# Two-phase MLPs after an attention: token and weight pieces queued half a step apart, some made a phase earlier

## The chip, the cores and the metric

The kernel runs on one core of one Trainium2 chip. The metric is the device time of one execution in microseconds (us). A core has the engines TensorE (PE, whose weight loads are listed as PEld), VectorE (DVE), ScalarE (ACT), GpSimd (POOL) and SyncE (SP). Each engine takes its own instructions in the order in which the program emits them, and here every DMA is issued by SP.

## The reference

Three stages follow each other. First comes an attention over 4 batches, 8 heads, 576 positions and 64 columns a head, with a bias that a small MLP makes from relative positions. Then two MLPs of 2304 tokens, 512 model columns and 2048 hidden columns, without residuals, all in float32:

```python
def _moe_ref(x, w_in, w_out):                 # layer 0
    h = x @ w_in
    g = h - np.tanh(h)
    return (g @ w_out).astype(np.float32)

def _moe2_ref(x, w_in, w_out, s, b):          # layer 1
    h = x @ w_in
    r = np.maximum(h, 0.0)
    g = s * (r * r) + b
    return (g @ w_out).astype(np.float32)
```

## The kernel before

Every instruction order is written out by hand: what is emitted first on an engine runs first there. A tile taken from a pool waits, in its first instruction, until the slot's last user is done.

**Attention** runs in 80 periods (`periods`, `NK`), one for a pair of heads, a batch and a block of 128 rows. In a period's end stand extra pieces from the table `work`: the weight steps of layer 0 for blocks u = 0 and 1 (`WK`, `WP`) and the tokens of batch 0 (`XK`, `XP`).

**First products.** Hidden columns are cut into 8 blocks (u) of 256, tokens into 4 batches (b) of 576. One pair (u, b) is an item. An item multiplies 2x2 blocks by Strassen's scheme with seven products P1 to P7 of 288 columns. Each product adds six matmuls: two halves j of the contraction, and three combinations of a high and a low part (a float32 is split into a rounded high part and the rest, hence "hi" and "lo", the second made by a subtraction). `first` gives two functions: `part0` emits P1, P6, P7 and the copy of P1 on ACT (L338) and two sums on DVE (L340, L342); `part1` emits P5, P2, P4, P3, the sums c22, c21 and c12 on DVE, the gates (`gate`, `gate2`) and two stores of g to DRAM (L362) on SP. Sums and gates live in the tile `ring`, a pool of 11 slots of 576 columns; products take turns in eight PSUM banks.

**Weights.** `step(layer, m, i)` makes one weight piece in five functions: `fetch` (SP loads 512 KB into the tile `stg`, three slots), `a` (ACT scales the high words, L108; DVE masks the sign, L109, into `wsg`), `b` (two DVE merges, L115 and L117, the last reader of `stg`), `c` (four DVE subtractions of 128 columns in the tile `wx`, for first weights only) and `d` (ACT writes the high part, POOL the low part; tiles `w` for first weights, `v` for second weights).

**Tokens.** `tokens(layer, b, j, e0, e1)` loads half j of a batch (L282), makes three more planes by subtraction (`s1`, `s2`, into the one slot of `xs`) and splits seven planes into high and low parts (tile `x`).

**Second products.** g is read back in 5 chunks of tokens (four of 512, one of 256); for each of 16 slices f, `load_g` (L594) loads 256 KB into a ring tile four steps ahead, `split_g` makes high (ACT, L600) and low parts two steps ahead into the pool `gp` of 14 slots, and `second` emits 12 matmuls (L620). In chunk 0 the low parts are POOL's, in the others DVE's. Second weights are made in the same steps, a slice each. After a chunk four banks are copied into ring tiles and stored (L624, L626).

The list `items` has, for each layer, 32 items and then 80 steps of second products; `pre[n]` lists the pieces emitted ahead of entry n. For a first-product entry, the first half of that list is emitted before `part0` and the second half between `part0` and `part1`. All pieces of a token half stand in one entry, those of batch b in entries 2b-2 and 2b-1 of the layer.

Of the kernel before, what the change touches and what calls it, by code (L numbers as in the profile page):

```python
# [10 lines left out]
F32 = mybir.dt.float32  # L11
# [17 lines left out]
NU = 8  # L29
# [21 lines left out]
XP = [("load", 0), ("s1", 2), ("h0", 3), ("h1", 4), ("l0", 4), ("l1", 5), ("l2", 6), ("s2", 7), ("h2", 7), ("l3", 8)]  # L51

GL, GS = 4, 2

@with_exitstack
def tile_kernel(ctx, tc, qk, vd, wcat, wts, sb, ltab, psib, ipsi8, out):
# [6 lines left out]
    wsg = ctx.enter_context(tc.tile_pool(name="wsg", bufs=1))  # L63
# [27 lines left out]
    raw_w, w1_t, w2_t, w2pool = {}, {}, {}, []  # L91

    def step(layer, m, i):
# [8 lines left out]
        def a():  # L102

            x = wst.tile([128, 8, 128], F32, tag="wx", name="wx")
            sg = wsg.tile([128, 512], I32, tag="wsg", name="wsg")
            hw = raw_w[key][:, 1]
            y = x[:, 0:4].rearrange("p n c -> p (n c)")
            nc.scalar.activation(out=y, in_=hw.bitcast(F32), func=AF.Copy, scale=2.0 ** -112)  # L108
            nc.vector.tensor_scalar(out=sg, in0=hw, scalar1=-2 ** 31, scalar2=1, op0=ALU.bitwise_and, op1=ALU.bitwise_or)  # L109
            raw_w[key] = (raw_w[key], x, y.bitcast(I32), sg)  # L110
# [9 lines left out]
        def c():  # L120
            x = raw_w[key][1]
            if m == 0:
                for o, y, z, op in ((4, 0, 3, ALU.add), (6, 1, 0, ALU.subtract), (5, 4, 1, ALU.subtract), (7, 2, 5, ALU.subtract)):
                    tt(nc.vector, x[:, o], x[:, y], x[:, z], op)

        def d():
# [5 lines left out]
            else:  # L132
                w = w2pool[i == NF - 1].tile([128, 2, 4, 128], F32R, tag=f"v{i}", name=f"v{i}")
# [134 lines left out]
    x_t, xpool, banks = {}, [xb0, None, None, None], []  # L268
# [4 lines left out]
    def tokens(layer, b, j, e0, e1):  # L273
# [3 lines left out]
        def load():  # L277
            r.append(xst.tile([128, 5, HT], F32, tag="xs", name="xs"))
            r.append(xpool[b].tile([128, 2, 7, HT], F32R, tag=f"x{b}{j}", name=f"x{b}{j}"))
            x_t[layer, b, j] = r[1]  # L280
# [15 lines left out]

        def lo(a, c, o, eng):
# [454 lines left out]
```

## Time and profile before

| | us |
|---|---|
| median of 2 runs (1314.87 to 1316.55) | 1315.71 |
| the profiled execution | 1315.19 |
| its span, first to last instruction | 1313.4 |
| PE busy | 1135.5 (86%) |
| DVE busy | 767.0 (58%) |
| ACT busy | 584.9 (45%) |
| POOL busy | 450.7 (34%) |

The stages of the span: bias table to 48 us, attention to 315.6, layer 0's items 1 to 31 to 587.4 (item 0 runs inside the end of attention), layer 0's second products to 811.3, layer 1's items to 1086.6 and its second products to 1309.8. A row of the timeline gives start, duration, engine, line, operation, the written tile, the read tiles, the shape and the count of instructions merged into it; in brackets stands the idle time before it and what ended it. `L85` is a helper that records all two-input operations, so these are told apart by tile. `PEclk` is the clock that TensorE was granted, as a share of the higher of its two levels.

### The profile page before, as it was taken

Reading aid. Unit: us, or ns where it says so; the run is one execution under the profiler, and the core shown is the slowest. Engines: PE = TensorE matmul, PEld = TensorE weight load, DVE = VectorE, ACT = ScalarE, POOL = GpSimd, SP = SyncE. Lnnn points to the kernel's source line nnn. Section 1 sums busy time; section 2 is a strip of 40 time slices with the busy share of each in tenths; the row PEclk is TensorE's granted clock in tenths of the full one; section 3 lists DMA queues with packets and bytes.
Section 4 is the critical chain, followed back from the end, with each engine's and each line's share of the span. In section 5 each row is a group of like instructions: output and inputs, shape, how many; then the busy total and the mean of one; then the engine's idle time right before and its main releaser. Section 6 shows DMA issues by size and latency. Waiting matters only on the chain. (4 is left out here: it accounts for less than half of the span.)

```text
span 1313.4 us, 21145 instructions
## 1 busy us (share of the span) xinstructions
PE 1135.5 (86%) x7624; PEld 901.3 (69%) x7624; DVE 767.0 (58%) x1598; ACT 584.9 (45%) x1178; POOL 450.7 (34%) x526
## 2 busy tenths in 40 slices
PE   9999999997546888888899998555888897799998
PEld 6455555555446888876588888445888796578887
DVE  8777777664235767787754322335778787832222
ACT  8877777773223333333433222222555464432122
POOL 0366566562335444557611110222211116700000
PEclk9999999999667999998999999776999998999999
DMA  8745353421213333465454313321333355444122
GB/s 285 246 128 206 111 189 106 147 84 59 101 56 102 124 122 105 139 202 186 154 192 178 130 35 114 104 72 59 116 139 123 123 195 193 156 161 160 60 85 96
DMA packets 81384, 175.36 MB, mean 134 GB/s; under 512 B 9472, under 2 KB 18560, under 8 KB 81280
## 3 DMA queue, kind: packets, MB, share of 16 engines
q1 hardware_dynamic: 81280, 174.01, 38.8%
q8 instruction: 60, 0.98, 0.3%
q14 instruction: 44, 0.36, 0.1%
HBM read 111.16 MB, written 62.82 MB: 132 GB/s over the span
## 5 line engine op out<-in xcount | busy, mean ns | idle before, releaser
L313 PE MATMUL h<-x,w 128*128 128x288 f32 x1356 | 226.2, 319 | 71.9 <-ACT ring L338 39.1
L313 PE MATMUL a<-x,w 128*128 128x288 f32 x1332 | 217.5, 315 | 67.9 <-ACT ring L338 39.0
L313 PEld LDWEIGHTS h<-x,w 128*128 128x128 f32 x1356 | 207.4, 209 | 81.1 <-ACT ring L338 42.0
L313 PEld LDWEIGHTS a<-x,w 128*128 128x128 f32 x1332 | 199.9, 205 | 75.9 <-ACT ring L338 41.8
L85 DVE TENSOR_TENSOR g<-ring,g 128x512 fp32r<-128x512 f32 (+1 forms) x128 | 87.0, 693 | 122.9 <-ACT g L600 122.5
L600 ACT CAST g<-ring 128x512 fp32r<-128x512 f32 (+1 forms) x160 | 90.0, 575 | 133.3 <-PE h L620 51.5
L452 POOL TENSOR_SCALAR pn<-p,sm 128x576 f32<-128x576 f32 (+2 forms) x208 | 125.2, 618 | 61.8 <-DVE sm L443 41.3
L85 POOL TENSOR_TENSOR w<-wx,w 128x896 fp32r<-128x896 f32 x32 | 67.8, 2122 | 191.6 <-ACT w L136 111.7
L620 PE MATMUL h<-v,g 128*128 128x512 f32 x432 | 118.3, 403 | 13.6 <-ACT g L600 7.9
L421 DVE CUSTOM_DVE_ANT_0 raw<-s,bias 128x576 f32<-128x576 f32 x144 | 103.9, 753 | 44.0 <-PE s L413 38.2
L620 PE MATMUL a<-g,v 128*128 128x512 f32 (+1 forms) x432 | 112.5, 389 | 14.5 <-POOL g L85 7.6
L85 DVE TENSOR_TENSOR ring<-h,ring 128x288 f32<-128x288 f32 x161 | 72.7, 455 | 84.4 <-ACT ring L338 45.4
L620 PE MATMUL h<-g,v 128*128 128x512 f32 (+1 forms) x528 | 121.2, 368 | 0.0
L85 DVE TENSOR_TENSOR ring<-a,ring 128x288 f32<-128x288 f32 x159 | 71.9, 455 | 78.7 <-ACT ring L338 37.4
L620 PE MATMUL a<-v,g 128*128 128x512 f32 x432 | 115.4, 401 | 0.0
L85 POOL TENSOR_TENSOR ring<-ring 128x576 f32<-128x576 f32 x64 | 74.5, 1184 | 116.2 <-ACT ring L318 54.7
L435 ACT ACTIVATE p<-raw,mn 128x576 f32<-128x576 f32 x144 | 110.6, 771 | 4.8 <-POOL pn L452 2.3
L620 PEld LDWEIGHTS h<-v,g 128*128 128x128 f32 x432 | 81.3, 190 | 40.4 <-ACT g L600 11.2
L620 PEld LDWEIGHTS a<-g,v 128*128 128x128 f32 x432 | 78.7, 189 | 38.0 <-POOL g L85 11.5
L620 PEld LDWEIGHTS h<-g,v 128*128 128x128 f32 x528 | 91.7, 190 | 17.9
L620 PEld LDWEIGHTS a<-v,g 128*128 128x128 f32 x432 | 82.6, 191 | 19.6
L462 PEld LDWEIGHTS t<-ident,pn 128*128 128x128 f32 (+1 forms) x656 | 69.7, 140 | 38.3 <-issue 20.6
(66 smaller groups left out, 1535.7 us busy)
## 6 DMA issues: line engine op xcount, KB each, us to landing
g_d<-ring SPq DMA_DIRECT2D x128, 288.0 KB, 2.5
stg<-in_wts SPq DMA_DIRECT2D x64, 512.0 KB, 4.0
ring<-g_d SPq DMA_DIRECT2D x128, 256.0 KB, 5.3
qk<-in_qk SPq DMA_DIRECT2D x16, 864.0 KB, 5.6
bias_d<-m SPq DMA_DIRECT2D x36, 296.0 KB, 4.5
bias<-bias_d SPq DMA_DIRECT2D x32, 288.0 KB, 4.7
xs<-x_d SPq DMA_DIRECT2D x32, 288.0 KB, 3.5
vv<-in_vd SPq DMA_DIRECT2D x16, 320.0 KB, 3.3
```

The source lines that it names most:

```text
L85: eng.tensor_tensor(out=out, in0=a, in1=b, op=op)
L313: nc.tensor.matmul(o, w[:, l, a], x[:, k, c], start=not add and j == 0 and m == 0, stop=j == 1 and m == 2, skip_group_check=add)
L421: nc.vector.tensor_tensor_reduce(out=raw.rearrange("p (c j) -> p c j", c=2), in0=s_t.pop((x, j))[:, :, 0:288], in1=bias_t[pairs[i][0], k]. ...
L435: nc.scalar.activation(out=p, in_=raw, func=AF.Exp, scale=-1.0, bias=mn, accum_out=sm[:, j:j + 1])
L452: nc.gpsimd.tensor_scalar(out=pn[:, c:c + b - a], in0=p[:, a:b], scalar1=sm[:, j:j + 1], scalar2=0.0, op0=ALU.mult, op1=ALU.add)
L462: nc.tensor.transpose(pm[0:c, j - g], pn[:, j * 128:j * 128 + c], ident)
L600: nc.scalar.copy(gh, g)
L620: nc.tensor.matmul(o, x, y, start=f == 0 and j == 0, stop=f == NF - 1 and j == 2)
```

## The change

Pieces are emitted at half steps: `pre[2n]` ahead of entry n, `pre[2n+1]` between `part0` and `part1`. Token pieces are fewer and larger (one `s`, two high parts, two low parts), one half step apart; the two subtracted planes that need extra room are put into a ring tile; `xs` has two slots. Half j = 0 of a batch is DVE's, j = 1 POOL's. Batch 1 of layer 0 is loaded and subtracted in attention's last periods, batches 0 and 1 of layer 1 are made whole, and batch 2 loaded and subtracted, in layer 0's second products. First weights for u = 2 are made up to `c` ahead of their layer, with `d` at half step 14 of it.

In a weight step the sign mask is written in place (it now follows ACT's reading of the same words), `wsg` is gone, the four subtractions of `c` are POOL's, two second-weight pieces share one `wx` tile, and `stg` has two slots; the last second-weight tile stands in a slot of `stg`.

Layer 1's gates are all a Relu on ACT, a square (DVE for "a", POOL for "b" and "c") and a scaling on POOL. High and low parts of g take ring tiles in place of the pool `gp`; loads of g go three steps ahead; in chunk 0 the low parts of odd f are DVE's.

```diff
-WK = [(0, 8), (1, 17), (2, 26), (3, 35)]
+WK = [(0, 8), (1, 17), (2, 26), (3, 35), (4, 52), (5, 60)]
-XK = [(0, 44), (1, 70)]
+XK = [(0, 63), (1, 71)]
+XP = {"load": 0, "s": 2, "h0": 3, "l0": 4, "h1": 5, "l1": 6}
-GL, GS = 4, 2
+GL, GS = 3, 2
...
-    stg = ctx.enter_context(tc.tile_pool(name="stg", bufs=3))
+    stg = ctx.enter_context(tc.tile_pool(name="stg", bufs=2))
-    xst = ctx.enter_context(tc.tile_pool(name="xst", bufs=1))
+    xst = ctx.enter_context(tc.tile_pool(name="xst", bufs=2))
...
-            x = wst.tile([128, 8, 128], F32, tag="wx", name="wx")
-            sg = wsg.tile([128, 512], I32, tag="wsg", name="wsg")
+            if m == 0 or i % 2 == 0:
+                x = w2x[0] = wst.tile([128, 8, 128], F32, tag="wx", name="wx")
+            else:
+                x = w2x[0][:, 4:8]
...
-            nc.vector.tensor_scalar(out=sg, in0=hw, scalar1=-2 ** 31, scalar2=1, op0=ALU.bitwise_and, op1=ALU.bitwise_or)
+            nc.vector.tensor_scalar(out=hw, in0=hw, scalar1=-2 ** 31, scalar2=1, op0=ALU.bitwise_and, op1=ALU.bitwise_or)
...
-                    tt(nc.vector, x[:, o], x[:, y], x[:, z], op)
+                    tt(nc.gpsimd, x[:, o], x[:, y], x[:, z], op)
...
+        def s():
+            x = r[0]
+            r.append(ring().rearrange("p (n c) -> p n c", n=2))
+            tt(eng, x[:, 4], x[:, 1], x[:, 0], ALU.subtract)
+            tt(eng, x[:, 1], x[:, 3], x[:, 1], ALU.subtract)
+            tt(eng, r[1][:, 1], x[:, 3], x[:, 4], ALU.subtract)
+            tt(eng, r[1][:, 0], r[1][:, 1], x[:, 2], ALU.subtract)
...
-                if name == "a":
-                    tt(nc.vector, g, h, g, ALU.mult)
-                nc.scalar.activation(out=g, in_=g, func=AF.Identity, scale=sb_t[:, 0:1], bias=sb_t[:, 1:2])
+                tt(nc.vector if name == "a" else nc.gpsimd, g, g, g, ALU.mult)
+                nc.gpsimd.tensor_scalar(out=g, in0=g, scalar1=sb_t[:, 0:1], scalar2=sb_t[:, 1:2], op0=ALU.mult, op1=ALU.add)
...
-            gh, gl = (gpool[0].tile([128, 512], F32R, tag="g", name="g")[:, 0:cn] for _ in range(2))
+            gh, gl = (ring(F32R)[:, 0:cn] for _ in range(2))
-            tt(nc.vector if c else nc.gpsimd, gl, g, gh.bitcast(F32), ALU.subtract)
+            tt(nc.vector if c or f % 2 else nc.gpsimd, gl, g, gh.bitcast(F32), ALU.subtract)
...
+            for q, (b, j) in enumerate((b, j) for b in range(2 + layer, B) for j in range(2)):
+                t = tokens(layer, b, j, (nc.vector, nc.gpsimd)[j])
+                for f, k in (("load", 0), ("s", 1), ("h0", 2), ("l0", 3), ("h1", 2), ("l1", 3)):
+                    add(2 * a0 + 2 + q // 2 * 4 + j + k, t[f])
...
+            for u in range(3, NU):
+                k = 2 * a0 + 8 * (u - 1)
+                for j, at in enumerate(((-6, -2, 0, 1, 3), (-3, 1, 3, 4, 6))):
+                    t = step(layer, 0, 2 * u + j)
+                    for f, n in zip(("fetch", "a", "b", "c", "d"), at):
+                        add(max(k + n, 2 * a0 + 14) if u == 3 and f == "a" else k + n, t[f])
...
+                    at = [2 * (f - n) for n in (5, 3, 2, 1)]
+                for p, n in zip(("fetch", "a", "b", "d"), at):
+                    order.append((k + n, "dba fetch".index(p), t[p]))
...
             if m == 0:
-                for f in fs[:len(fs) // 2]:
-                    f()
                 part0, part1 = first(layer, x, y, lambda: bank()[:, 0:HT])
                 part0()
-                for f in fs[len(fs) // 2:]:
+                for f in pre.pop(2 * n + 1, []):
                     f()
                 part1()
```

## Rows read from the trace of the kernel before

**Rows 1.** Busy time by stage: us, then each engine's busy us and instructions.

```profile
315.60:420.00 104.40, 55.71 (x276) 52.02 (x275) 38.02 (x76) 26.16 (x47) 37.85 (x36) 0.67 0.25 85
420.00:587.40 167.40, 145.63 (x1030) 141.10 (x1028) 121.39 (x228) 63.12 (x124) 84.47 (x63) 0.97 0.40 138
587.40:654.00 66.60, 52.14 (x192) 37.21 (x193) 51.81 (x43) 26.74 (x49) 47.06 (x32) 0.92 0.49 165
...
811.30:925.00 113.70, 63.13 (x322) 59.71 (x321) 47.90 (x96) 34.84 (x59) 25.40 (x25) 0.74 0.25 83
925.00:1086.60 161.60, 142.78 (x1026) 137.99 (x1025) 127.05 (x277) 86.37 (x149) 27.44 (x14) 0.99 0.41 143
1086.60:1152.50 65.90, 52.34 (x193) 36.73 (x194) 51.19 (x45) 27.63 (x50) 44.59 (x30) 0.95 0.49 162
```

The columns are PE, PEld, DVE, ACT, POOL, then the granted clock, the share of the DMA engines and GB/s.

**Rows 2.** Timeline of layer 0's head, three rows of SP, DVE and PE.

```profile
316.92 10.46 SPq L282 DMA_DIRECT2D xs<-x_d  x4
...
320.19 0.46 DVE L85 TENSOR_TENSOR xs<-xs 128x288 f32<-128x288 f32 x1 [3.96 <-DMA xs<-x_d]
...
326.12 1.81 PE L313 MATMUL a<-x,w 128*128 128x288 f32 x6 [7.05 <-ACT ring L338]
```

**Rows 3.** Timeline of layer 0's steady items, one turn, all engines.

```profile
447.93 1.75 PE L313 MATMUL h<-x,w 128*128 128x288 f32 x12
...
449.52 0.96 PE L313 MATMUL a<-x,w 128*128 128x288 f32 x6
...
458.16 2.87 DVE L85 TENSOR_TENSOR wx<-wx 128x128 f32<-128x128 f32 x4
458.21 2.34 POOL L85 TENSOR_TENSOR ring<-ring 128x576 f32<-128x576 f32 x2 [3.26 <-DMA g_d<-ring]
...
462.35 1.06 PE L313 MATMUL h<-x,w 128*128 128x288 f32 x6 [1.45 <-ACT ring L338]
...
466.43 1.36 PE L313 MATMUL h<-x,w 128*128 128x288 f32 x6 [2.22 <-DVE ring L85]
```

**Rows 4.** Timeline of layer 1's items, where POOL has no gates.

```profile
936.66 1.02 DVE L85 TENSOR_TENSOR wx<-wx 128x128 f32<-128x128 f32 x4
```

**Rows 5.** Timeline of layer 0's chunk 0, ACT.

```profile
616.45 0.67 ACT L108 ACTIVATE wx<-stg 128x512 f32<-128x512 f32 x1 [2.58 <-POOL v L85]
```

**Rows 6.** Groups by line and shape, whole span: count, busy us, mean ns, idle before.

```profile
L600 ACT CAST g<-ring 128x512 fp32r<-128x512 f32 x128 | 77.6, 617 | 108.5 <-PE h L620 44.2 <-PE a L620 32.6 <-DMA ring<-g_d 31.0
L85 DVE TENSOR_TENSOR g<-ring,g 128x512 fp32r<-128x512 f32 x96 | 74.1, 783 | 99.8 <-ACT g L600 99.6
L85 POOL TENSOR_TENSOR w<-wx,w 128x896 fp32r<-128x896 f32 x32 | 67.8, 2122 | 191.6 <-ACT w L136 111.7 <-PE a L313 31.5 <-PE h L313 25.8
L452 POOL TENSOR_SCALAR pn<-p,sm 128x576 f32<-128x576 f32 x80 | 60.0, 750 | 61.8 <-DVE sm L443 41.3 <-PE t L462 13.4 <-DVE pt L474 3.2
L85 POOL TENSOR_TENSOR ring<-ring 128x576 f32<-128x576 f32 x32 | 47.7, 1492 | 116.2 <-ACT ring L318 54.7 <-issue 45.6 <-DMA g_d<-ring 15.8
L85 POOL TENSOR_TENSOR ring<-ring 128x288 f32<-128x288 f32 x32 | 28.1, 877 | 0.0
L452 POOL TENSOR_SCALAR pn<-p,sm 128x64 f32<-128x64 f32 x64 | 22.0, 344 | 0.0
```

**Rows 7.** The same groups in 593 to 652 us, then in 652 to 811 us.

```profile
L117 DVE SCALAR_TENSOR_TENSOR wx<-stg,wx 128x512 int32<-128x512 int32 x12 | 20.2, 1685 | 0.4
...
L117 DVE SCALAR_TENSOR_TENSOR wx<-stg,wx 128x512 int32<-128x512 int32 x4 | 2.8, 692 | 0.1
```

**Rows 8.** Timeline of POOL at the end of layer 0's items.

```profile
588.39 2.60 POOL L85 TENSOR_TENSOR ring<-ring 128x576 f32<-128x576 f32 x2 [2.78 <-DMA g_d<-ring]
```

**Rows 9.** Waits of SP's queue in 594 to 652 us: total, times, longest.

```profile
SPq L99 <- DVE wx L117: 31.5, 9, 6.0
```

**Rows 10.** DMA issues in 600 to 650 us: count, size, median us to landing.

```profile
ring<-g_d SPq DMA_DIRECT2D x14, 256.0 KB, 4.1
```

**Rows 11.** Timeline of attention, PE behind a low part on POOL.

```profile
153.52 0.87 PE L462 MATMUL t<-ident,pn 128*128 128x128 f32 x6 [0.72 <-DVE pt L474]
```

More of the change, by code (lines that the diff above doesn't have):

```diff
@@ L265, in tile_kernel, with tokens @@
         del bq[:9]
-    x_t, xpool, banks = {}, [xb0, None, None, None], []
+    x_t, xpool, banks, staged, xstaged = {}, [xb0, None, None, None], [], [], []
     def ring(dtype=F32):
         return bp.tile([128, S], dtype, tag="bias", name="ring")
-    def tokens(layer, b, j, e0, e1):
+    def tokens(layer, b, j, eng):
         r = []
@@ L385, in tile_kernel @@
             pieces = step(0, 0, i)
+            if i >= 4:
+                staged.append(pieces["d"])
             for f, k in WP.items():
-                work.setdefault(n + k, []).append(pieces[f])
-        for j, n in XK:
-            pieces = tokens(0, 0, j, nc.gpsimd, nc.vector)
-            for f, k in XP:
-                work.setdefault(n + k, []).append(pieces[f])
+                if i < 4 or f != "d":
+                    work.setdefault(n + k, []).append(pieces[f])
+        for j, n in XK:
+            pieces = tokens(0, 0, j, nc.vector)
+            for f, k in XP.items():
+                work.setdefault(n + k, []).append(pieces[f])
+        for j in range(2):
+            pieces = tokens(0, 1, j, (nc.vector, nc.gpsimd)[j])
+            xstaged.append(pieces)
+            for f, k in (("load", -1), ("s", 3)):
+                work.setdefault(NK + j + k, []).append(pieces[f])
         for i in range(2, len(pairs)):
@@ L638, in tile_kernel @@
             items += [(layer, 0, NU - 1, b) for b in (2, 3, 1, 0)]
-            b0 = base[layer, 1] = len(items)
+            b0 = len(items)
             items += [(layer, 1, c, f) for c in range(len(CHUNKS)) for f in range(NF)]
+            add(2 * a0, open_x)
             post[b0 - 3] = open_w2
-            post[b0 - 1] = open_g
-            post[len(items) - 1] = close_second
-            add(a0, open_x)
-            for b in range(1, B):
-                for j in range(2):
-                    t = tokens(layer, b, j, *((nc.vector, nc.vector) if j == 0 else (nc.gpsimd, nc.gpsimd)))
-                    for f in XP:
-                        add(a0 + 2 * b - 2 + j, t[f[0]])
@@ L654, in tile_kernel @@
+            for f in staged:
+                add(2 * a0 + 14, f)
+            staged, xstaged = [], []
+            for u in range(3, NU):
+                k = 2 * a0 + 8 * (u - 1)
+                for j, at in enumerate(((-6, -2, 0, 1, 3), (-3, 1, 3, 4, 6))):
                     t = step(layer, 0, 2 * u + j)
-                    add(k + j - (2 if u > 2 else 3), t["fetch"])
-                    for f, n in (("a", 0), ("b", 0), ("c", 1), ("d", 1)):
-                        add(a0 + 7 if u == 2 and f == "d" else k + j + n, t[f])
+                    for f, n in zip(("fetch", "a", "b", "c", "d"), at):
+                        add(max(k + n, 2 * a0 + 14) if u == 3 and f == "a" else k + n, t[f])
@@ L669, in tile_kernel @@
                     t = step(1, 0, i)
-                    for p, k in (("fetch", -3), ("a", 0), ("b", 1), ("c", 2), ("d", 3)):
-                        add(b0 + 20 + 4 * i + k, t[p])
+                    if i >= 4:
+                        staged.append(t["d"])
+                    for p, k in WP.items():
+                        if i < 4 or p != "d":
+                            add(2 * (b0 + (18 + 4 * i if i < 4 else 54 + 4 * i) + k), t[p])
+                for b, j, k in ((0, 0, 38), (0, 1, 44), (1, 0, 52), (1, 1, 58)):
+                    t = tokens(1, b, j, nc.gpsimd)
+                    for p, n in XP.items():
+                        add(2 * (b0 + k + n), t[p])
@@ L689, in tile_kernel @@
             else:
-                for f in fs:
-                    f()
                 second(layer, x, y)
```

92 lines of the change are left out of this document (39 added, 53 removed).

## The prediction

> **What bounds the kernel now.** I read the busy time by stage first [rows 1]. TensorE (PE) does the work of every stage, so I compare its busy time with the least it could need. Dense first products take 1.59 us per 12 matmuls, 0.1325 us each [rows 3]; an item (one pair of feature blocks u, one batch b: 7 products of 6 matmuls) thus needs 5.57 us, 31 items 172.5 us, 32 items 178 us. Layer 0's items 1 to 31 take 271.8 us (315.6 to 587.4), layer 1's 32 take 275.3 us (811.3 to 1086.6): some 196 us of loss. It sits mostly in the heads, where the first row of each layer shows 276 and 322 matmuls (37 and 43 us at full speed) in 104 and 114 us, at a granted clock of 0.67 and 0.74. The first 16 second products of a layer, chunk 0, take 66 us with the hand-over, against 16 x 2.8 = 45 us; the 64 after them run 654 to 811.3 us, which is dense.
>
> Then the cause of each loss. In the head [rows 2] DVE's first token subtraction waits for its load, 3.3 us after issue. All ten token pieces of one half stand in one item's queue, so ACT comes late to the copy (L338) that PE waits for, and PE has stood 7.05 us. In the steady items a turn of four (one u, 168 matmuls) takes 167.4 x 168 / 1030 = 27.3 us instead of 22.3 [rows 1]: two waits, 1.45 and 2.22 us, and matmuls at a lower clock behind them (the six at 466.43 us take 1.36 us) [rows 3]. The cause stands ahead of them: four weight subtractions on DVE hold it 2.87 us while POOL runs a 2.34 us gate pair; the same four take 1.02 us where POOL idles [rows 4]. In chunk 0 ACT's weight piece waits 2.58 us a step for POOL's w-low [rows 5], and 16 steps take 66.6 us, 4.2 each.
>
> **The change, part by part.** The sum is made against the profiled run's own 1315.2 us (span 1313.4 and 1.8 outside it), 0.5 us under the median of 1315.7.
>
> *Layer 0's items, 271.8 us to 200.* Batch 1's tokens are subtracted during attention's last periods; those of 2 and 3 are spread over half steps. Walked through with row durations, three things are late next. The subtraction of batch 2 (first half) sits on DVE before item 1's c22 and waits for its load: 2.6 us. Batch 3's load stands on SP behind item 2's stores, these behind POOL's gates, these behind ACT, which waits for POOL's 4 x 0.88 us token subtraction [rows 6]; DVE stops ahead of item 3's c22: 5.8 us. The halves made on POOL then delay items 4 to 6 by 0.7, 2 and 1.4 us; with the staged weight casts I take 15 us, and 4 for matmuls at the lower clock. In the steady turns the four subtractions leave DVE for POOL. What is left is the two-piece merge (L115, L117, 0.69 us each clean [rows 7]) ahead of a c22 that had 0.8 us to spare: 0.5 to 1.5 us a turn; six turns, 9 us. 172.5 + 15 + 4 + 9 = 200. Lower end 183 (stalls hidden by the eight banks), upper 221 (steady turns as now).
>
> *Layer 1's items: POOL becomes the bound.* Its busy time before is 27.4 of 161.6 us [rows 1]. After, each item puts on it a 576-wide and a 288-wide square (1.49 + 0.88) and three scalings (0.75 for 576; 0.54 each for two of 288, an estimate between 0.34 for 64 and 0.75) [rows 6]: 4.2 us, 134 us for 32. Ten weight pieces cost 2.12 for the low part and four subtractions of 128 columns, not seen on POOL: from 0.34 (64 wide, one input) to 0.88 (288 wide); I take 0.58, on the line between them: 4.4 us, 44 in all. Two staged low parts 4, token halves 5 + 8 (1440-wide ones scaled from the 896-wide row), W2's first four 6. Together 202 us against PE's 178. POOL also waits some 11 us at the start (first gate, a token load behind SP's stores, a half-built token), and I add 5 us for meeting DVE. So POOL ends 218 us after layer 1's start. Batches 0 and 1 being ready saves the head, but PE then waits for ring slots. Bounds: 190 (squares at the pair's 2.34 us of [rows 3], the small scalings and subtractions at 0.34: 179 and 11) to 261 (the port, below).
>
> DVE beside a busy POOL is where the shared port matters: [rows 3] against [rows 4], 2.87 to 1.02 us for the same four instructions.
> The Trainium skill's page "SBUF — State Buffer", section "Who interferes with whom", says that a VectorE instruction with two SBUF inputs and a GpSimd instruction that reads SBUF exclude each other for a whole instruction; the trace agrees, with those 2.87 us beside a 2.34 us pair. It speaks against this change, which fills POOL in layer 1: by the rule the sum would be rival 2's 1237 us, by the row, in which POOL lost nothing, 1194.
>
> *Chunk 0, 63 us to 64 from POOL's last gate (590.95 us in [rows 8]) to chunk 1's start (654.0).* Removed: the wait for w-low, since two W2 pieces now share one wx tile and odd slices' low halves go to DVE. Put in its place: stg has two slots, not three, and the fetch of piece m+2 is queued on SP ahead of g(m) but needs the slot that merge m frees. SP already waits there, 31.5 us in nine waits [rows 9], yet its g loads had two steps to spare; now g(m) leaves only once merge m is done. For odd m DVE stands on it: issue 0.45, landing 4.1 [rows 10], cast 0.62, low part 0.78 [rows 6], next merge 1.4: 7.4 us; for even m the low part is POOL's and the next merge follows in 1.9. Two steps take 9.3 us, 4.65 each, no better than 4.2. Start 7.3, four long and five short links 39, tail 14: 60, and 4 for port meetings. Bounds: 50 (fetch wait not binding) to 77 (merge and mask at L117's 1.69 us [rows 7]).
>
> *Chunks 1 to 4:* high and low parts now share the ring of 11 slots with raw loads (3 tiles a step) and loads go three steps ahead, not four. A load behind a chunk's four stores leaves some 2.6 us late; with 4.1 + 1.4 us it has 8.4: hidden, else 1 us a chunk end. I take 2 us a layer, ends 0 and 8.
>
> *Attention, +5 us.* Six steps put four subtractions (2.3 us) on POOL; a 2.1 us low part there makes PE wait 0.72 us [rows 11]. So 6 x 0.8. The in-place mask now waits for ACT and tokens move to DVE, both under PE's full rows. Ends 0 and 12.
>
> Sum: attention +5; layer 0's items -71.8, chunk 0 +1, chunks +2; layer 1 from 811.3 to chunk 1's start at 1152.5, 341.2 us before, 218 + 64 = 282 after, -59.2; chunks +2. That is -121: 1315.2 - 121 = 1194 us.
>
> **Rivals.**
> 1. *Forecast, 1194 us, 0.47*: heads gone, layer 1 at POOL's pace.
> 2. *The port at full price, 0.2.* Every two-input DVE instruction in layer 1 holds POOL for its own time: one square of 0.45 an item and six of 0.69 per four items, 1.5 us x 32 = 48, of which 5 are counted: 1237 us. For it: [rows 3] against [rows 4]. Against: in [rows 3] DVE paid and POOL did not, its pair of 2.34 us is no longer than the mean of 2.37 [rows 6].
> 3. *PE bound in both layers, 0.2.* POOL at its lower ends gives layer 1 190 instead of 218, layer 0's items 190: 1194 - 28 - 10 = 1156 us.
> 4. *The heads stay, 0.08.* Token loads queue on SP behind stores that wait for POOL, as now for L338's sake; heads win half: +45 for layer 0, +45 for layer 1 with its longer POOL tail: 1284 us. Against: two batches need no load at the start of layer 1.
> 5. *Slower: the ring starves the second products, 0.05.* With raw, high, low, four outputs at a chunk end and a token tile on 11 slots, a load's real lead shrinks to one step: 0.45 + 4.1 + 1.4 = 5.95 us a step instead of 2.8, over the 128 steps of chunks 1 to 4: +400, 1594 us. At two steps' lead it is 2.98 and +23 us. Slower than before from (1315 - 1194)/128 = 0.95 us a step, a lead under 1.6 steps. Against: high and low need 1.5 to 2 steps each, raw 2.4, together some 6 slots.
>
> **How the numbers follow.** The likeliest is 1, 1194 us, its own range 1160 to 1225 us from the ends of its parts, which seldom all fall one way. The range 1150 to 1240 takes in 1, most of 2 and 3, some 0.8 in all. About 2% is what can be told from no change: 1289 to 1342 us. Faster: 1, 2, 3 and half of 4, 0.9; same: half of 4 and mild cases of 5, 0.05; slower: 5, 0.05.
>
> **What would show it.** Right: POOL over 90% busy in layer 1's items, PE idle ended by ring tiles there; no token wait of PE over 6 us; four subtractions absent from DVE; chunk 0's steps in pairs of 9 to 11 us, SP's longest waits at L99 for the merge; chunks 1 to 4 still 157 us. Wrong: POOL's 128-wide subtractions far from 0.58 us, squares far from 1.49, layer 1's items at 178 us, or gaps in chunks 1 to 4.

## The result and the profile after

The changed kernel took 1240.3 us (median of two runs, 1238.64 to 1241.96) against 1315.7: a ratio of 0.943, 95% interval [0.937, 0.949]. The forecast was 1194 us, in a range of 1150 to 1240. The direction was right, but the gain came to 75 us where 121 were forecast.

Some words for what follows: the head of a layer is its first items, up to where the turns settle (the rows below take it to 420 us in layer 0 and 874 in layer 1); the steady items are those behind it, in turns of four; the hand-over is the stretch from the last first product to the first second product; a raw load brings a slice of g back before it is split into high and low part.

The profiled execution took 1241.96 us with a span of 1240.2. Busy time by stage of the changed kernel, with the columns of [rows 1]; the stages shown are layer 0's head, its chunk 0 and its chunk 4, then layer 1's head, steady items and chunk 0:

```profile
315.90:420.00 104.10, 83.29 (x543) 80.36 (x541) 61.38 (x105) 41.47 (x71) 69.66 (x60) 0.89 0.36 123
...
533.40:610.80 77.40, 57.63 (x194) 41.88 (x193) 37.78 (x48) 25.92 (x46) 31.08 (x23) 0.85 0.43 143
...
745.00:775.70 30.70, 26.23 (x194) 24.62 (x193) 14.33 (x27) 7.26 (x19) 7.03 (x12) 0.94 0.49 159
775.70:874.00 98.30, 83.91 (x584) 82.21 (x582) 53.73 (x101) 38.73 (x72) 79.71 (x89) 0.93 0.32 112
874.00:998.70 124.70, 108.43 (x764) 104.78 (x763) 79.10 (x142) 47.34 (x93) 111.46 (x132) 0.97 0.41 141
998.70:1079.50 80.80, 57.96 (x192) 43.43 (x193) 37.26 (x48) 25.89 (x47) 31.91 (x25) 0.81 0.42 137
```

The first row stands against 315.6 to 420 of [rows 1]: almost the same time, but 543 matmuls instead of 276. The heads gave the gain. The rows of chunk 0 took some of it back: it takes, with its hand-over, 77.4 and 80.8 us where it took 66.6 and 65.9, with TensorE busy only 57.6 of 77.4 us. And chunk 4 takes 30.7 us (745 to 775.7), with TensorE busy for 26.2, where the kernel before took 23.0 without a gap.

Against the terms of the forecast, from the same end points:

| term | forecast | measured | difference |
|---|---|---|---|
| attention | +5 | +0.3 | -4.7 |
| layer 0's items (to PE's last product) | 200 | 217.5 | +17.5 |
| from there to POOL's last gate | 3.6 | 2.8 | -0.8 |
| layer 0's chunk 0, from POOL's last gate | 64 | 74.6 | +10.6 |
| layer 0's chunks 1 to 4 | 159.3 | 164.9 | +5.6 |
| layer 1's items, to POOL's end | 218 | 227.5 | +9.5 |
| layer 1's chunk 0, from POOL's end | 64 | 76.3 | +12.3 |
| layer 1's chunks 1 to 4 | +2 | 0 | -2 |

The differences add up to 48 us, which is 1242 against 1194.

Chunk 0's loop in the changed kernel, from its timeline over all engines (on SP's queue L98 is a weight fetch and L586 a raw gate load; on DVE L116 and L118 are the merge and L110 the mask; on ACT L592 is the high part of a gate; L84 are all two-input operations of DVE and POOL):

```profile
569.00 0.69 DVE L118 SCALAR_TENSOR_TENSOR wx<-stg,wx 128x512 int32<-128x512 int32 x1
...
569.72 0.33 SPq L98 DMA_DIRECT2D stg<-in_wts  x1
...
570.15 0.38 SPq L586 DMA_DIRECT2D ring<-g_d  x1
...
575.65 0.50 PE L612 MATMUL a<-ring,v 128*128 128x512 f32 x1 [0.91 <-POOL v L84]
...
575.76 0.62 ACT L592 CAST ring<-ring 128x512 fp32r<-128x512 f32 x1 [1.84 <-DMA ring<-g_d]
...
576.47 0.69 DVE L84 TENSOR_TENSOR ring<-ring 128x512 fp32r<-128x512 f32 x1 [2.00 <-ACT ring L592]
...
576.98 1.32 POOL L84 TENSOR_TENSOR v<-wx,v 128x512 fp32r<-128x512 f32 x1 [1.38 <-ACT v L139]
577.08 1.77 DVE L116 SCALAR_TENSOR_TENSOR wx<-wx,stg 128x512 int32<-128x512 int32 x1
578.88 0.69 DVE L118 SCALAR_TENSOR_TENSOR wx<-stg,wx 128x512 int32<-128x512 int32 x1
...
579.60 0.33 SPq L98 DMA_DIRECT2D stg<-in_wts  x1
...
587.32 0.80 PE L612 MATMUL a<-ring,v 128*128 128x512 f32 x1 [0.91 <-POOL v L84]
```

It is the closed loop of the forecast: a merge ends at 569.69, SP issues the fetch that waited for it and then the raw load; the raw data is there at 575.76, and only behind its high and low part comes the next merge. The end of one merge to the end of the next long one is 9.9 us (569.69 to 579.57), two steps together 11.67 (575.65 to 587.32). Between 545.10 and 593.13 us four such long links and five short ones take 48.0 us. SP's longest waits between 536 and 610 us, against the 31.5 us of [rows 9], and below them ScalarE's wait for raw loads in the same stretch:

```profile
SPq L98 <- DVE stg L110: 38.9, 5, 8.5
...
SPq L98 <- DVE wx L118: 4.5, 5, 0.9
...
ACT ring L592 <- DMA ring<-g_d: 38.5, 10, 6.4
```

By time the profile lays SP's wait to the mask (L110) of a conversion and not to its merge. But each of the ten fetches from 545 us on leaves 0.03 us behind the end of a second merge (L118), as at 569.69 and 569.72 or 579.57 and 579.60: it is the merge that sets it free.

### The profile page after: what moved, and what is told of

It is laid out like the page before. It is cut to its first block, busy times and chain, and to the rows that moved or that the text cites. A ratio compares the mean times of both kernels' runs of the same rounds, so it can differ in the third digit from the quotient of the medians.

```text
span 1240.2 us, 21386 instructions
## 1 busy us (share of the span) xinstructions
PE 1122.2 (90%) x7624; PEld 891.9 (72%) x7624; DVE 693.3 (56%) x1408; ACT 554.0 (45%) x1130; POOL 624.7 (50%) x780
## 5 line engine op out<-in xcount | busy, mean ns | idle before, releaser
L84 DVE TENSOR_TENSOR ring<-ring 128x512 fp32r<-128x512 f32 (+2 forms) x176 | 122.8, 701 | 245.6 <-ACT ring L592 217.8
L84 POOL TENSOR_TENSOR ring<-ring 128x576 f32<-128x576 f32 (+2 forms) x144 | 162.9, 1141 | 155.3 <-ACT ring L320 75.3
L592 ACT CAST ring<-ring 128x512 fp32r<-128x512 f32 (+1 forms) x160 | 91.6, 577 | 305.6 <-DMA ring<-g_d 238.4
L316 PEld LDWEIGHTS h<-x,w 128*128 128x128 f32 x1356 | 194.5, 196 | 32.7 <-DVE ring L84 23.6
L612 PE MATMUL h<-v,ring 128*128 128x512 f32 x405 | 112.1, 407 | 22.9 <-ACT v L139 9.2
L612 PE MATMUL a<-ring,v 128*128 128x512 f32 (+1 forms) x405 | 109.7, 398 | 24.2 <-ACT v L139 8.6
L612 PE MATMUL h<-ring,v 128*128 128x512 f32 (+1 forms) x495 | 119.0, 381 | 0.0
L612 PE MATMUL a<-v,ring 128*128 128x512 f32 x405 | 114.1, 417 | 0.0
L612 PEld LDWEIGHTS h<-v,ring 128*128 128x128 f32 x405 | 77.4, 193 | 46.1 <-ACT v L139 11.0
L612 PEld LDWEIGHTS h<-ring,v 128*128 128x128 f32 x495 | 90.2, 200 | 17.6
L84 DVE TENSOR_TENSOR ring<-h,ring 128x288 f32<-128x288 f32 x145 | 65.8, 455 | 55.5 <-PE h L316 37.5
L612 PEld LDWEIGHTS a<-v,ring 128*128 128x128 f32 x405 | 81.7, 202 | 20.3
L497 PE MATMUL o<-pt,vv 128*64 128x256 f32 (+1 forms) x640 | 95.0, 418 | 0.0
```

The costliest lines, as they stand in the source:

```text
L84: eng.tensor_tensor(out=out, in0=a, in1=b, op=op)
L316: nc.tensor.matmul(o, w[:, l, a], x[:, k, c], start=not add and j == 0 and m == 0, stop=j == 1 and m == 2, skip_group_check=add)
L497: nc.tensor.matmul(o[h], v[:, e, j], unit_t[i, u][:, 4 if j == 4 else 5 * e + j, 0:n], start=(j == 0), stop=(j == 4))
L592: nc.scalar.copy(gh, g)
L612: nc.tensor.matmul(o, x, y, start=f == 0 and j == 0, stop=f == NF - 1 and j == 2)
```

## The experiments

Stage lengths are worked out from each trace: from the first matmul of one kind of product to the first of the next (the hand-over's last TensorE work counts with the items), a chunk from its first matmul to the next chunk's. The kernel of each row but the first two is told of below.

| kernel | us | layer 0: items | chunk 0 | chunk 4 | layer 1: items | chunk 0 |
|---|---|---|---|---|---|---|
| before | 1315.7 | 290.1 | 60.4 | 23.0 | 281.0 | 60.1 |
| changed | 1240.3 | 231.8 | 75.2 | 30.7 | 225.1 | 78.8 |
| e1_fetch_later | 1206.8 | 229.9 | 59.4 | 29.9 | 222.7 | 62.6 |
| e8_raw_act_queue | 1241.0 | 231.2 | 61.8 | 40.2 | 223.3 | 62.8 |
| e1b_lead4 | 1202.8 | 230.4 | 56.7 | 26.6 | 228.1 | 60.0 |
| e4_head_lead5 | 1181.7 | 223.0 | 57.4 | 23.7 | 217.4 | 59.4 |
| e2_c_dve | 1252.9 | 234.6 | 76.9 | 30.8 | 231.3 | 76.8 |
| e3_scale_act | 1272.6 | 229.4 | 74.7 | 30.6 | 261.4 | 74.6 |
| e5_d_earlier | 1203.7 | 231.4 | 57.7 | 27.0 | 222.7 | 60.1 |
| e6_gates_before | 1203.8 | 231.7 | 57.0 | 26.8 | 235.1 | 58.7 |
| e7_whole_steps | 1214.8 | 236.7 | 60.0 | 26.9 | 232.0 | 59.9 |
| e9_layer1_late | 1200.3 | 222.2 | 57.6 | 22.7 | 236.7 | 60.4 |
| e10_tokens_dve | 1190.0 | 223.2 | 57.4 | 23.6 | 219.7 | 59.9 |
| e11_h_later | 1187.1 | 222.2 | 59.1 | 23.4 | 219.5 | 59.1 |
| e12_no_wlo | 1160.4 | 213.4 | 57.9 | 23.4 | 203.9 | 61.6 |
| e13_wlo_dve | 1165.0 | 219.3 | 59.8 | 24.3 | 205.7 | 62.7 |

Layer 1's items differ by 5 us between e1b_lead4, e1_fetch_later and e5_d_earlier, whose edits hardly touch them; a difference of that size there decides nothing.

### Chunk 0: what the raw load waits for

```diff
-                    at = [2 * (f - n) for n in (5, 3, 2, 1)]
+                    at = [2 * (f - n) for n in (4, 3, 2, 1)]
```

> Only edit: each fetch of second-product weights is issued one step later (four steps ahead instead of five), behind the merge that frees its staging buffer, so that SP no longer sits on that merge with a raw gate load queued behind it. Theory Q (SP's queue sets chunk 0: the raw load lands 5.6 us after it can be issued and is issued only when its split is due): the two stretches of chunk 0 with their hand-overs, 77.4 and 80.8 us in the changed kernel, fall to 60 to 68 each, and the whole to 1208 to 1222 us. Rival D (VectorE's merges slowed beside GpSimd, 1.77 us, and its masks and subtractions set the step): the stretches stay at 74 us or more each, the whole at 1232 to 1243. Rival F (a fetch lands too late for its own conversion when it has one step less): the stretches grow, the whole 1245 or more.

1206.8 us, ratio 0.918 [0.916, 0.920] to the kernel before. Chunk 0 went from 75.2 to 59.4 us and from 78.8 to 62.6. ScalarE's waits in this kernel's chunk 0 (534 to 594 us), and the first row of TensorE after a wait in three double steps:

```profile
ACT wx L109 <- DMA stg<-in_wts: 23.0, 10, 4.1
...
ACT ring L592 <- DMA ring<-g_d: 1.3, 1, 1.3
...
557.12 0.50 PE L612 MATMUL a<-ring,v 128*128 128x512 f32 x1 [0.71 <-POOL v L84]
...
564.31 0.50 PE L612 MATMUL a<-ring,v 128*128 128x512 f32 x1 [1.17 <-POOL v L84]
...
571.29 0.50 PE L612 MATMUL a<-ring,v 128*128 128x512 f32 x1 [0.79 <-POOL v L84]
```

Two steps take 7.0 to 7.2 us now, and ScalarE waits for raw loads 1.3 us in all, not 38.5. SP still waits for a merge ahead of each fetch, but for one that comes a step earlier in the order, so the raw load behind it is no longer held up. Rival D falls: the merges still meet GpSimd, and the stage is shorter. Rival F's time falls too, but its wait is there: ScalarE now stands 23.0 us on weight fetches, which it did not do in the changed kernel. No run here took that wait away. The whole came out just below theory Q's range.

The same could have come from bandwidth, since a fetch moved later no longer travels beside the raw load. So the other way round, fetches as they were and raw loads on another queue:

```diff
-            nc.sync.dma_start(out=t, in_=g_d[layer][f][:, c0:c0 + cn])
+            nc.scalar.dma_start(out=t, in_=g_d[layer][f][:, c0:c0 + cn])
```

> The changed kernel with one edit: the raw gate loads are issued by ScalarE instead of SP; fetches, leads and order as they were. It separates two readings of why the later fetch helped. Theory Q1 (SP's order: the raw load stood on SP behind a fetch that waits for a merge): the raw loads no longer pass SP, chunk 0's two stretches fall from 75 and 79 us to 58 to 66, the whole to 1208 to 1222. Theory Q2 (bandwidth: a raw load lands 5.6 us after its issue since 512 KB fetches are under way at the same time): the fetches are where they were, so the stretches stay at 72 to 80 and the whole at 1232 to 1243.

The two stretches that decide fell to 61.8 and 62.8 us, within theory Q1's 58 to 66. The whole stayed at 1241.0 us, which was expected of Q2: all that chunk 0 won was lost elsewhere, chunk 4 took 40.2 us instead of 30.7, layer 0's chunks 1 to 3 9 us more in all, and layer 1's last chunk, to its last matmul, 33.5 us instead of 22.4. There the load is issued behind ScalarE's own casts, as two neighbouring rows of this kernel's chunk 4 show:

```profile
751.75 0.41 ACT L592 CAST ring<-ring 128x256 fp32r<-128x256 f32 x1 [3.51 <-DMA ring<-g_d]
751.83 0.33 ACTq L586 DMA_DIRECT2D ring<-g_d  x1
```

Each load leaves only when the cast that waits for an older load has started: the same fault on another queue. The stage tells Q1 from Q2; the total alone would have told the wrong one. The run does not hold the bandwidth quite fixed, since the raw loads, which no longer leave right behind two fetches, landed after 2.6 to 4.2 us (542 to 592 us) instead of 3.7 to 5.7. But in the changed kernel the load of each long link took 5.1 to 5.7 us against the 4.1 of the kernel before: over four links that is some 5 of the 13 to 16 us.

Then the lead of the kernel before, on top of the later fetch:

```diff
-GL, GS = 3, 2
+GL, GS = 4, 2
```

> The later fetch and also raw gate loads four steps ahead instead of three (the lead that the kernel before had). Theory Q: if one step more of lead for the raw loads is not enough with the later fetch alone, this gives the rest: the stretches of chunk 0 at 58 to 66 us and the whole at 1200 to 1216; chunk 4 of layer 0 (30.7 us) falls to 26 to 28 too, since the raw loads have four steps of 1.44 us to land. Rival D: the whole at 1228 to 1243, the stretches of chunk 0 unchanged from the run with the later fetch alone.

1202.8 us, 0.915 [0.912, 0.918], all as theory Q had it. Chunk 0 lost another 2.7 and 2.6 us, chunk 4 of layer 0 went to 26.6. That is not yet the 23.0 of the kernel before, which had the same four steps; why it needed no fifth was not looked into. The cause in chunk 4 stands in the changed kernel's rows: a step is 1.44 us there, and the cast waits for its load before TensorE waits for the cast.

```profile
770.65 0.74 ACT L592 CAST ring<-ring 128x256 fp32r<-128x256 f32 x2 [4.85 <-DMA ring<-g_d]
...
771.11 1.25 PE L612 MATMUL a<-ring,v 128*128 128x256 f32 x3 [2.20 <-ACT ring L592]
```

### The heads

```diff
-                for f, k in (("load", 0), ("s", 1), ("h0", 2), ("l0", 3), ("h1", 2), ("l1", 3)):
+                for f, k in (("load", 0), ("s", 2), ("h0", 3), ("l0", 4), ("h1", 3), ("l1", 4)):
...
-                add(2 * (b0 + k - GL), lambda a=(layer, c, f): load_g(*a))
+                add(2 * (b0 + k - GL - (c == 4)), lambda a=(layer, c, f): load_g(*a))
```

> On top of the later fetch with raw loads four steps ahead (1202.8 us): two edits in stages that do not touch. In the head of each layer's items the token subtractions and everything behind them come one half step (about 3 us) later, so that their load has two half steps to land instead of one; and the raw gate loads of chunk 4 go five steps ahead instead of four. Theory: the two longest waits of the heads (5.2 us in layer 0 and 5.75 us in layer 1, TensorE on a VectorE subtraction that waits for its load, issued behind stores on SP) are VectorE standing on a load, and what stood behind it on VectorE was late with it: each layer's items lose 4 to 8 us (230 and 228 us now), chunk 4 of layer 0 goes from 26.6 to 23 to 25.5, the whole 1186 to 1196. Rival: the tokens themselves are what TensorE lacks there, so coming later makes the wait longer: items the same or up to 6 us longer, the whole 1199 to 1210.

1181.7 us, 0.899 [0.896, 0.902]: below both ranges. Items lost 7.4 and 10.7 us (the second with the 5 us of scatter named above), chunk 4 came to 23.7 (23.0 before). The wait that went, first in the changed kernel:

```profile
331.75 10.41 SPq L359 DMA_DIRECT2D g_d<-ring  x4
...
342.27 3.11 SPq L283 DMA_DIRECT2D xs<-x_d  x4
...
346.13 0.46 DVE L84 TENSOR_TENSOR xs<-xs 128x288 f32<-128x288 f32 x1 [4.54 <-DMA xs<-x_d]
...
348.67 3.25 PE L316 MATMUL h<-x,w 128*128 128x288 f32 x12 [5.22 <-DVE ring L84]
```

and in this version, where the load again stands behind stores, but DVE does its combinations first:

```profile
339.54 3.07 SPq L283 DMA_DIRECT2D xs<-x_d  x4
...
343.07 0.46 DVE L84 TENSOR_TENSOR xs<-xs 128x288 f32<-128x288 f32 x1 [2.06 <-DMA xs<-x_d]
...
348.74 1.06 PE L316 MATMUL a<-x,w 128*128 128x288 f32 x6 [1.81 <-DVE ring L84]
```

Two more attempts on the same heads, each on top of this version; the first gives the odd token halves to VectorE (`nc.vector` for `(nc.vector, nc.gpsimd)[j]`), the second starts the rounding of the staged halves later (`2 * a0 + j + k + 1 + layer`).

> On top of the 1181.7 us version: the odd token halves of the items' heads are subtracted and rounded by VectorE instead of GpSimd. Theory (the two engines exclude each other: a 0.46 us subtraction of VectorE took 2.88 us beside GpSimd's 3.29 us one): a half costs GpSimd 8.3 to 9.6 us, much of which VectorE stands still, and VectorE itself 4.2 us, so each layer's items lose 2 to 7 us (223 and 217 now), the whole 1168 to 1180. Rival: VectorE, 65% busy there, is late with its combinations then, items 3 to 10 us longer, the whole 1187 to 1202.

> On top of the 1181.7 us version: the rounding of the token halves that were staged before the items starts one half step later in layer 0 and two in layer 1, with the batches behind it two half steps later in layer 1. Theory: the two waits of 3.4 and 2.7 us in layer 0's head and the one of 5.2 us in layer 1's, in which TensorE waits for a ScalarE copy that is queued behind a token rounding whose operand GpSimd has not made yet, shrink: items 3 to 6 us shorter in each layer, the whole 1170 to 1177. Rival: the tokens are then late for their own item, as far as they were early: 1180 to 1190.

1190.0 us, 0.906 [0.902, 0.909], and 1187.1, 0.904 [0.902, 0.907]: both a little slower than the version they build on, with stages within 3 us of it. Both theories fall, which had the items shorter. The totals lie in the ranges of the rivals, but the items grew by 2.3 us at most, where the first rival had 3 to 10, so the rivals' reasons are not shown either.

### The steady items: VectorE beside GpSimd

The changed kernel's turn of four items takes 24.5 us in layer 0 (forecast 23.8), with one wait:

```profile
391.67 2.12 POOL L84 TENSOR_TENSOR w<-wx,w 128x896 fp32r<-128x896 f32 x1
...
391.83 2.51 DVE L116 SCALAR_TENSOR_TENSOR wx<-wx,stg 128x512 int32<-128x512 int32 x1
394.37 0.69 DVE L118 SCALAR_TENSOR_TENSOR wx<-stg,wx 128x512 int32<-128x512 int32 x1
...
395.48 0.80 PE L316 MATMUL a<-x,w 128*128 128x288 f32 x4 [1.66 <-DVE ring L84]
```

Queueing that subtraction one half step earlier (`((-6, -2, 0, 1, 2), ...)` for `((-6, -2, 0, 1, 3), ...)`) did not help:

> On top of the later fetch with raw loads four steps ahead (1202.8 us): the rounding of the even weight of a pair (ScalarE copy, then GpSimd's 2.12 us subtraction) is queued one half step earlier, so that GpSimd's subtraction no longer stands in the half step of the odd weight's merges on VectorE. Theory: the merge of 2.5 us beside that subtraction goes back to 1.0 to 1.3 us, the one wait of 1.6 us in each turn of layer 0 goes, turn 24.5 to 23 to 23.6 us, each layer's items 4 to 8 us shorter, the whole 1188 to 1198. Rival: the subtraction then slows another VectorE operation as much, turn 24 to 25, the whole 1199 to 1207.

1203.7 us, 0.916 [0.912, 0.919]; layer 0's turn is still 24.5 us (443.58 to 468.10) with a wait of 1.6. That is the rival's time, but the rows show that the edit did not do what it was for. The merge still meets the same subtraction, which stands on GpSimd behind the same pair of gates:

```profile
439.75 2.13 POOL L84 TENSOR_TENSOR w<-wx,w 128x896 fp32r<-128x896 f32 x1
...
440.25 2.18 DVE L116 SCALAR_TENSOR_TENSOR wx<-wx,stg 128x512 int32<-128x512 int32 x1
```

So this run tests neither reading, and the subtraction was taken away, and then given to VectorE, on top of the 1181.7 us version:

```diff
-            tt(nc.gpsimd, w[:, 1], x, w[:, 0].bitcast(F32), ALU.subtract)
+            if m == 0:
+                nc.scalar.copy(w[:, 1], x)
+            else:
+                tt(nc.gpsimd, w[:, 1], x, w[:, 0].bitcast(F32), ALU.subtract)
```

```diff
-            tt(nc.gpsimd, w[:, 1], x, w[:, 0].bitcast(F32), ALU.subtract)
+            tt(nc.gpsimd if m else nc.vector, w[:, 1], x, w[:, 0].bitcast(F32), ALU.subtract)
```

> On top of the 1181.7 us version, with a part of the computation left out: the low half of every first-layer weight is not subtracted by GpSimd but written as a second copy of the high half by ScalarE, so that GpSimd's 2.12 us subtraction is gone and ScalarE has 0.93 us more per weight. Theory (VectorE's merge, 0.68 us alone and 2.46 beside that subtraction, is late and with it the combination that TensorE waits for, 1.6 us in each turn): merges at 0.7 us, no wait in the steady turns of layer 0, which go from 24.5 to 22.8 to 23.3 us; items of layer 0 from 223 to 211 to 217 us. Rival: the wait is that of VectorE's own queue (merges, mask and combinations in a row) and stays, turn 24 or more, items 220 or more.

> On top of the 1181.7 us version: VectorE subtracts the first-layer weights' low halves instead of GpSimd (all is computed). Theory (the two exclude each other on these operands): VectorE pays some 1.0 us for what cost it up to 1.8 us of standing still, so layer 0's turn stays within 23.3 to 24.6 us and layer 1's, where GpSimd is 90% busy, gains 0.5 to 1.5 us a turn: the whole 1168 to 1181. Rival: VectorE's queue is what TensorE waits for, each turn 1 to 2 us longer, the whole 1190 to 1205.

Without it the first merge (L116) of layer 0's steady items takes 0.68 to 0.86 us (least, median and longest in ns). The second one (L118) of the other weight still takes 1.8 beside GpSimd's gates, as it did in the changed kernel, and costs TensorE nothing: no wait for VectorE is left in the turn of 23.46 us:

```profile
L116 DVE SCALAR_TENSOR_TENSOR wx<-wx,stg x10: 681/682/861, 440.8 to 524.1; 128x512 int32<-128x512 int32 x10
L118 DVE SCALAR_TENSOR_TENSOR wx<-stg,wx x10: 692/1736/1810, 441.5 to 524.9; 128x512 int32<-128x512 int32 x10
...
437.61 1.07 PE L319 MATMUL a<-x,w 128*128 128x288 f32 x6 [0.36 <-ACT ring L338]
461.07 1.07 PE L319 MATMUL h<-x,w 128*128 128x288 f32 x6 [0.36 <-ACT ring L338]
```

So the merge that the subtraction slows is the cause of the 1.6 us. The turn is 1.1 us shorter, with 0.36 us now lost to ScalarE; it ends 0.2 us above the theory's bound, the items at 213.4 us within it. On VectorE the subtraction takes 1.13 us, layer 0's turn stays at 24.6 (454.19 to 478.75 us, with two waits of 0.70 and 0.84) and layer 1's falls from 25.9 to 24.3. Layer 1's waits, the changed kernel's first, then this version's:

```profile
885.60 1.06 PE L316 MATMUL a<-x,w 128*128 128x288 f32 x6 [0.86 <-ACT ring L335]
890.16 0.40 PE L316 MATMUL h<-x,w 128*128 128x288 f32 x1 [1.17 <-POOL w L84]
900.84 1.06 PE L316 MATMUL h<-x,w 128*128 128x288 f32 x6 [0.68 <-DVE ring L84]
```

```profile
L84 DVE TENSOR_TENSOR w<-wx,w 128x896 fp32r<-128x896 f32 x6 | 6.8, 1128 | 4.1 <-ACT w L139 4.1
...
852.87 1.06 PE L316 MATMUL h<-x,w 128*128 128x288 f32 x6 [1.18 <-DVE ring L84]
877.21 1.06 PE L316 MATMUL a<-x,w 128*128 128x288 f32 x6 [1.21 <-DVE ring L84]
```

The three waits in a turn have become one. With 1165.0 us (1163.7 to 1169.5), 0.886 [0.884, 0.889], this is the fastest version that computes everything, a little below the theory's range; it is 75 us below the changed kernel.

### What each part of the change is worth

Four more runs undo a part. On the changed kernel itself, the four subtractions of `c` back on VectorE, and layer 1's scaling back on ScalarE:

> The four 128-wide combinations of a first-layer weight go back from GpSimd to VectorE; all else as in the changed kernel. Theory: GpSimd is near its limit in layer 1's items only (busy 111 of 125 us) and VectorE's merges are near it in layer 0's. So layer 0's steady turn (24.5 us) grows by 1 to 3 us, its items by 4 to 10, and layer 1's turn (25.9) falls by 0.5 to 1.5 us, its items by 2 to 6: the whole at 1236 to 1248. Rival (moving the combinations off VectorE is what gave the items their whole gain): layer 0's turn back to 27 or more, the whole at 1255 or more.

> Layer 1's scaling of the gates goes from GpSimd to ScalarE (three per item, 0.57 to 1.14 us each on GpSimd); all else as in the changed kernel. Theory P (GpSimd sets layer 1's items): its turn of four items falls from 25.9 to 23.8 to 24.8 us, the stretch of the items from 223 to 209 to 215, the whole to 1226 to 1233. Rival (GpSimd's load is hidden, the items wait for loads and for VectorE): the stretch stays at 219 to 227, the whole at 1236 to 1245.

The first: 1252.9 us, 0.952 [0.948, 0.955], between the two ranges. Layer 0's items grew by 2.8 us, less than expected; layer 1's grew by 6.2 where a fall was expected. Its turn did fall by 0.2 us (934.20 to 959.85 against 900.84 to 926.70), but its head has 552 matmuls in the first 98.3 us where the changed kernel has 584. Moving `c` is worth 12.6 us of the 75 by the medians, not the bulk.

The second: 1272.6 us, 0.968 [0.966, 0.970], against both theories: the items of layer 1 took 261 us instead of 225. ScalarE's groups in 870 to 1000 us of this kernel tell why (count, busy us, mean ns, idle before and its cause):

```profile
L327 ACT ACTIVATE ring<-ring,sb_t 128x288 f32<-128x288 f32 x32 | 19.9, 623 | 25.4 <-DVE ring L84 24.6 <-POOL ring L84 0.8
L327 ACT ACTIVATE ring<-ring,sb_t 128x576 f32<-128x576 f32 x16 | 13.9, 870 | 12.5 <-POOL ring L84 12.4
```

ScalarE is busy 72 us of 130, yet stands 38 us on squares of other engines, with the next gate and the next item's copy queued behind. GpSimd was busy in 111 of 125 us in the changed kernel; relieving it at that place cost more than it gave. With the gates as a whole as before (two of the three squares on VectorE out of the operand, in front of the scaling), on top of e1b_lead4:

> On top of the later fetch with raw loads four steps ahead (1202.8 us): layer 1's gates as the kernel before had them (two of three gates squared by VectorE out of the operand, scaled by ScalarE), the rest unchanged. Theory: the change's own gates gave layer 1 something, since they take three scalings off ScalarE's queue, which stood 38 us of 130 on products of GpSimd and VectorE when they were put back: layer 1's items grow from 228 to 236 to 262, the whole 1211 to 1237. Rival: with the squares on VectorE instead of GpSimd ScalarE does not stand, GpSimd is relieved by 4 us per item and the items fall to 214 to 226, the whole 1188 to 1200.

1203.8 us, 0.917 [0.913, 0.920], between the two ranges: no difference that can be told. Layer 1's items are 7 us longer in the profile, hardly more than their scatter. The new gates bring little by themselves.

The two halves of the change's name: half steps undone (the middle bundle moved ahead of `part0()`), on top of e1b_lead4, and for layer 1 alone the second batch of tokens and the third unit's weights made in the items again, on top of e4_head_lead5:

> On top of the later fetch with raw loads four steps ahead (1202.8 us): the pieces that are queued in the middle of an item of first products are queued at its start with the others, all in the same order; nothing else. Theory: spreading the pieces by half steps is worth 1 to 3 us of each turn of four items (waits of VectorE on POOL and ScalarE inside one bundle), so items of 230 and 228 us grow by 8 to 20 each, the whole 1218 to 1242. Rival: the order is what counts, not the half step, the whole 1199 to 1210.

> On top of the version with the tokens a half step later and chunk 4's loads five steps ahead (1181.7 us): for layer 1 alone, the second batch of tokens and the weights of the third unit are no longer made during layer 0's second products but inside layer 1's items, as the kernel before did. Theory: the second products have the room (VectorE 35 to 45% and GpSimd 30 to 40% busy there) and the head of the items has none, so layer 1's items grow from 217 to 227 to 245 us and nothing else changes: the whole 1191 to 1210. Rival: the head waits for other things anyway, the items 213 to 221, the whole 1178 to 1186.

1214.8 us, 0.924 [0.922, 0.926], and 1200.3, 0.914 [0.912, 0.915]. The half steps are worth 12 us, from 6.3 and 3.9 in the items and 3.3 in chunk 0, less than expected. Making the first tokens and weights early is worth 19.3 us in layer 1's items, within the theory's bounds, and layer 0's second products, which took the work in, are only 0.8 us longer for it (215.3 against 214.5 us). Layer 1's items fell by 56 us in all; the parts undone one at a time (19.3, 7.0, 6.2 and 3.9 us) make 36 of them, two of these near the scatter. The rest, to which two token buffers and the spread of the batches belong, was not taken apart.

## Why the prediction was partly right

**Right: where the gain is.** The heads went from 276 matmuls in 104.4 us to 543 in 104.1, and from 322 in 113.7 to 584 in 98.3. No wait for a token is over 6 us (5.22 and 5.75 are the longest). Attention lost nothing: GpSimd's four subtractions take 1.83 us there instead of 2.3, and no wait of TensorE came with them.

**Chunk 0: the mechanism was named, its long link was too short.** The step that failed is "issue 0.45, landing 4.1 [rows 10], cast 0.62, low part 0.78, next merge 1.4: 7.4 us". Measured, the long link is 9.9 us and the short one 1.8 (forecast 1.9). The landing was 5.6 us (570.15 to 575.76), with two fetches of 512 KB and another raw load issued in the 2.2 us before it: 1.5 more. The merge behind it took 2.46 us beside GpSimd's low part instead of 1.4: 1.1 more. The other links are 0.2 less in all, which makes 9.3 + 2.4 = 11.7 us for two steps, as measured. So the loop took 48.0 us where the sum had 39; start and tail took 5.3 more than their 7.3 and 14. The 4 us put by for port meetings happen to be about what four slow merges cost; nothing was put by for the landing, taken at a median of other loads, in a loop that sends two fetches ahead of it every time. The loop was also called nearly free, "no better than 4.2", where the order of two lines of issue was worth 16 us in each layer.

**Layer 0's items: the head was sized too small, in part for the token load.** From 315.9 to 395.5 us 374 matmuls, 49.6 us when dense, took 79.6: a loss of 30 us where the sum had 15 + 4 = 19. Behind it the loss was 15 us where the sum had 9. The forecast had this wait ("Batch 3's load stands on SP behind item 2's stores", 5.8 us; measured 5.22). e4_head_lead5 cut it to 1.81, 3.4 us less, and the items lost 7.4: by the difference, what stands behind it was late with it, which the sum left out. The rest of the head's overrun was not taken apart. The steady turn was 24.5 instead of 23.8 us, since "0.69 us each clean" did not hold for the merge, at 2.51 beside GpSimd; e12_no_wlo shows that this is the wait. That run took in all 9.6 us from the items.

**Chunk 4 of layer 0: a step length that was overlooked.** "With 4.1 + 1.4 us it has 8.4: hidden" is right for steps of 2.8 us. Chunk 4's are 1.44 us, so three steps ahead are 4.3. It cost 7.7 us; two steps more of lead gave 7.0 back.

**Layer 1's items: POOL near its bound, but not the bound alone.** The term that failed is POOL's waiting. Its work from 775.7 to its last gate at 1003.2 us came to 194.9 us, where the sum had 202; its idle time came to 32.6, where the sum had 11 and 5. Most of that is the scaling of gate "a", which waits for VectorE's square:

```profile
POOL ring L327 <- DVE ring L84: 19.6, 9, 6.4
```

What makes that square late was not taken apart. POOL was 81% busy in the head and 89% behind it, so close to the "over 90%" that was to show it; TensorE waited 1.17 us a turn for it, for a weight and not for a ring tile as the forecast had it, and 1.54 for ACT and DVE. Its prices were good but for one, 0.95 us for a 576-wide scaling (0.75): 2.10 us for a low part (2.12), 1.28 for a 576-wide square (1.49), 0.46 for a 128-wide subtraction (0.58), 0.68 for a 288-wide scaling (0.54).

**Rival 2's time was met, its mechanism only in part.** It gives 1237 us for POOL losing 48 us to VectorE in layer 1. Those items took 9.5 us more than forecast, and chunk 0's queue order took more than that. The rows show losses on both sides: VectorE at 754.02 us and POOL at 766.15 us in e4_head_lead5, each behind the other's longer operation:

```profile
753.30 3.29 POOL L84 TENSOR_TENSOR x<-xs,x 128x1440 fp32r<-128x1440 f32 x1
...
754.02 2.88 DVE L84 TENSOR_TENSOR ring<-ring 128x288 f32<-128x288 f32 x1 [0.80 <-ACT ring L320]
...
765.45 2.23 DVE L84 TENSOR_TENSOR x<-xs,x 128x1440 fp32r<-128x1440 f32 x1
...
766.15 2.57 POOL L327 TENSOR_SCALAR ring<-ring,sb_t 128x288 f32<-128x288 f32 x1
```

A VectorE square of 0.46 us (the expectation of e10_tokens_dve calls it a subtraction) took 2.88 and ended 0.3 us behind GpSimd's; a GpSimd scaling of 0.58 us took 2.57 and ended 1.0 us behind VectorE's. In both, whoever came second waited.
The Trainium skill's page "SBUF — State Buffer", section "Who interferes with whom", states just that: the order of issue decides who blocks, and for the whole instruction. These rows agree.

**The other rivals.** The heads did not stay (rival 4), though a token load behind stores did hold up each of them, TensorE did not become the bound in the items (rival 3), and chunks 1 to 3 and all of layer 1's later chunks stayed dense on the ring of 11 (rival 5).

## What to carry to other kernels

Where a queue in order carries both a transfer that waits for a slot and one that does not, write the order of issue out for two turns of the loop: here a fetch issued one step before its slot was free held up every load behind it, 16 us in each of two stages, and the same happened on ScalarE's queue when the loads were put there. In such a loop take each link's price as it is at that place, next to what the loop itself starts at that moment, not from a median of other rows or an undisturbed one. And judge an experiment by the stage that it edits: e8_raw_act_queue left the total where it was while it won 13 to 16 us in each of the two stages in question.

## What the runs showed of the hardware

VectorE and GpSimd cost each other more than the busy shares suggest: a merge of 0.68 us took 2.51, a square of 0.46 us 2.88, and a GpSimd scaling of 0.58 us 2.57. Taking one GpSimd subtraction of 2.1 us per weight away gave 9.6 and 13.5 us in the two layers' items; giving it to VectorE, where it takes 1.13 us, still gave 3.7 and 11.7 (layer 1's with a scatter of 5).

A 256 KB load landed in a median of 4.1 to 4.2 us from its issue in both kernels' chunk 0, but in 5.1 to 5.7 in the changed kernel's long links, where two fetches of 512 KB and another load were issued within the 2.2 us before it.
